# Attention into two gated layers on one core: the first pair's preparation split and fused, turns of an identity ahead of it, the Newton seed on GpSimd, a new table of attention and new last stores

## The chip, the cores and the metric

The kernel runs on one core of one Trainium2 chip. The metric is the device time of one launch in microseconds (us), lower is better; the times shown are the median of three runs, with the lowest and the highest.

## What is computed

```
rmsnorm(x, g) = x / sqrt(mean(x*x) + 1e-6) * g
scores = 1/sqrt(64) * rmsnorm(q, g_q) @ rmsnorm(k, g_k).T      # 4 batches, 12 heads, 448 x 64
attn   = exp(scores - rowmax);  attn /= sum(attn) + 1e-9
x = heads side by side of (attn @ v)                           # 1792 x 768
h = x @ moe_w_in;   x = (h * sigmoid(h)) @ moe_w_out           # 768 -> 2048 -> 768
h = x @ moe2_w_in;  out = (max(h, 0)**2) @ moe2_w_out          # 768 -> 2048 -> 768
```

Everything is float32; the weights arrive as 8-byte floats and are rebuilt into 4-byte ones by bit operations.

## The kernel before

**Stages.** Attention works on 24 pairs of heads, one after the other. `prepare` loads q and k of a pair, squares them (ScalarE, L571), sums the squares (VectorE, L580), finds the inverse root by three Newton rounds from a seed made of the bits of the number (L589 to L625), multiplies (`norm`, L634), turns the result by TensorE transposes (`turn_q`, L646) and cuts it into an upper and a lower part (`q_hi`, L655 and L657, on ScalarE; `q_lo`, L662 and L664, on VectorE). For the first pair the Newton steps run on VectorE, for all others on GpSimd, except the two seed steps L596 and L603, which are always VectorE's. `weigh` makes for each quarter of the rows, or chunk, the score products of both heads (L699), the row maxima (L710), the exponentials (L717), the turn of these (`turn_e`, L726) and a copy out of PSUM (`e_copy`, L525 on ScalarE or L527 on VectorE). `attend` inverts the sums (L746, L747), multiplies with v (L775) and copies the result out of the one PSUM bank `pv` (`pv_copy`, L525). Then layer one (up and down, L1002, L1089, L1186) and layer two (L1089, L1436, L1558), each partly with seven products in place of eight, and the stores of the output (L1422).

**Array forms.** The score products take 64 rows of the array each, so the two heads stand above each other and run at once. The products with v fill 64 columns each and stand side by side. The turns and all products of the layers use the whole array.

**Order.** All work is listed first as steps with the engines that may do them; a planner (`Plan`) then issues them. Attention's steps have fixed times, `nominal`, which is the pair's number times `PERIOD`, plus an entry of `TABLE`, plus for the first four pairs an entry of `FIRST`; on each engine they are issued in the order of these times. All other steps (the loading and splitting of weights, the layers, the stores) go between them where the planner's model finds room, ranked by due times that `DUE` shifts by kind and stage. The numbers end as nothing but the order of each engine's instructions: each engine runs its list in order, and a wait holds back everything behind it.

```
    at = PERIOD * i + {**LOADS, **TABLE}[kind][n] + (FIRST[i][kind][n] if kind in FIRST.get(i, ()) else 0.0)
```

Of the kernel before, what the change touches and what calls it, by code (L numbers as in the profile page):

```python
# [15 lines left out]
P = 128  # L16
# [19 lines left out]
ECOPY = [[("dve",), ("act",)], [("act",), ("dve",)]] * 2  # L36


PERIOD = 10.424
FIT = 0.1  # L40
QUIET = 24.0
LOADS = {
    "load_g": [-27.0], "gains": [-3.0], "load_qk": [-46.9, -46.4], "load_v": [-10.0],
# [3 lines left out]
    "squares": [-25.39, -24.85],  # L47
    "sums": [-21.96],
    "newton": [-18.58, -15.46, -15.21, -14.73, -14.37, -14.0, -13.64, -13.27, -12.91, -12.54, -12.18, -11.81, -11.45, -11.08, -10.72],
    "norm": [-10.35, -7.85],  # L50
    "turn_q": [-8.3, -3.09],
    "q_hi": [-7.71, -2.41],
    "q_lo": [-6.6, -1.71],
    "scores": [0.0, 0.61, 5.21, 5.82],
    "row_max": [0.82, 1.67, 2.75, 2.21, 6.03, 6.57, 7.64, 7.1],
    "exp": [1.47, 3.15, 4.84, 3.76, 6.97, 8.01, 9.77, 9.16],
    "turn_e": [4.25, 4.64, 6.57, 6.95, 9.47, 9.85, 11.78, 12.16],
    "e_copy": [4.85, 5.45, 7.58, 8.18, 11.02, 10.44, 12.82, 14.02],
    "attend": [13.07, 18.28],
    "pv_copy": [21.35],  # L60
    "inverse": [12.09],
    "attended": [22.08],
    "x_hi": [25.45],
    "x_lo": [26.04],
}
FIRST = {
    0: {"squares": [13.08, 13.26], "sums": [11.05], "newton": [8.9, 6.09, 6.15, 7.01, 6.96, 6.9, 6.85, 6.79, 6.79, 6.73, 6.68, 6.67, 6.62, 6.56, 6.51], "norm": [6.45, 4.56], "turn_q": [5.13, 0.65], "q_hi": [5.48, 0.91], "q_lo": [5.05, 0.87], "scores": [-0.12, 0.42, 0.35, 0.89], "row_max": [0.42, 0.11, 1.77, 1.24, 0.89, 0.89, 1.5, 1.5], "exp": [0.43, 0.54, 0.34, 0.55, 0.61, 0.19, 0.22, 0.22], "turn_e": [-1.2, 0.0, 1.44, 1.79, -0.0, 0.0, -0.0, 0.0], "e_copy": [0.21, 0.88, 1.37, 1.5, -0.81, 0.17, -0.31, -0.31], "pv_copy": [0.08], "inverse": [-0.31], "attended": [-0.09], "x_hi": [-0.23], "x_lo": [-0.23]},
    1: {"squares": [4.86, 4.86], "sums": [2.68], "newton": [0.55, -1.24, -0.51, -0.72, -0.71, -0.72, -0.71, -0.72, -0.71, -0.72, -0.71, -0.72, -0.71, -0.72, -0.71], "norm": [0.29, -2.82], "turn_q": [0.2, -3.55], "q_hi": [0.55, -2.22], "q_lo": [0.16, -0.71], "exp": [0.0, -0.0, -0.46, 0.0, 0.72, 0.72, 0.19, 0.19], "turn_e": [0.0, -0.0, 0.38, 0.38, -0.0, 0.0, -0.0, 0.0], "e_copy": [-0.0, -0.22, 0.72, 0.6, -0.58, 0.14, -0.31, -0.31], "pv_copy": [0.23], "inverse": [-0.31], "attended": [0.06], "x_hi": [4.34], "x_lo": [8.92]},
    2: {"squares": [-3.56, -0.81], "sums": [-1.57], "newton": [-2.97, 0.21, 0.21, -0.0, 0.0, -0.0, 0.0, -0.0, 0.0, -0.0, 0.0, -0.0, 0.0, -0.0, 0.24], "norm": [0.24, -1.21], "turn_q": [-0.0, -0.77], "q_hi": [0.0, -0.85], "q_lo": [-0.0, -0.53], "exp": [0.0, -0.0, -0.0, 0.0, -0.0, 0.88, 0.35, 0.34], "e_copy": [-0.0, 0.0, 0.88, -0.0, -0.58, 0.29, -0.31, -0.31], "pv_copy": [0.13], "inverse": [-0.31], "attended": [-0.04], "x_hi": [-0.23], "x_lo": [-0.23]},
# [53 lines left out]
class Plan:  # L123
# [82 lines left out]
    def forward(self, due, end=None):  # L206
# [20 lines left out]
        while len(order) < len(steps):  # L227
            best = None
            for e in ENGINES:
                f = free[e]  # L230
                next = fixed[e][-1] if fixed[e] else None
                for n in wait[e]:
# [170 lines left out]
def kernel(  # L403
# [46 lines left out]
    def sa(shape, dt, tag, n=None):  # L450
        return sb(shape, dt, tag, n, "ap")
# [1213 lines left out]
```

## Time and profile before

| | |
|---|---|
| median of three runs (lowest to highest) | 1171.79 us (1171.0 to 1171.94) |
| time of the profiled execution | 1172.46 us |
| span of its trace, first to last instruction | 1170.6 us |
| TensorE busy | 1147.3 us, 98% |
| VectorE, ScalarE, GpSimd busy | 986.7, 577.7, 298.1 us |
| mean DMA rate | 197 GB/s |

The trace has a line for every instruction with its start and duration. Tile names: `T` holds the split q and k, `n` the normalized ones before the turn, `s`, `t` and `pv` are PSUM banks, `E` the exponentials, `PT` the turned ones, `gg` in the last stage the running sum of the output. PE is TensorE's products, PEld its weight loads, DVE VectorE, ACT ScalarE, POOL GpSimd, SP the engine that issues all DMAs. One fp32 turn or product of v shows as one or two instructions of the array. A line of the timeline that ends in xN is N instructions of one form in a row.

### The profile page before, as it was taken

The page shows a single profiled execution, that of the slowest core. Times are in us where ns is not written, and L with a number is a line of the kernel's source. Part 1 is how long each engine was busy: PE and PEld are TensorE (multiplying, and loading weights), DVE is VectorE, ACT ScalarE, POOL GpSimd, SP SyncE. Part 2 cuts the span into 40 slices and gives each one's busy share as a digit, 9 for nine tenths or more (in the row PEclk, how much of TensorE's full clock was granted, in tenths as well). Part 3 has the DMA queues.
Part 4 walks back from the last instruction along what each step waited for, and adds up shares of the span by engine and source line. Part 5 has one row for each costly group of instructions (what it writes and reads, how often), then busy time and mean ns, then how long its engine had stood idle before and what let it go on. Part 6 is the DMA issues. An engine that isn't in the chain of part 4 may idle for free.

```text
span 1170.6 us, 19174 instructions
## 1 busy us (share of the span) xinstructions
PE 1147.3 (98%) x6825; PEld 1022.6 (87%) x6825; DVE 986.7 (84%) x1737; ACT 577.7 (49%) x1205; POOL 298.1 (25%) x487
## 2 busy tenths in 40 slices
PE   5999999999999999999999999999999999999998
PEld 3777777778899999999999998999999998999997
DVE  7999999887999998995588899678788876888876
ACT  5999999884343333432334353544433534333321
POOL 3566766541000000110010012122341310232220
PEclk9999999999999999999999999999999999999999
DMA  7555547637898888752265839888768795555444
GB/s 172 85 80 92 88 87 108 100 54 175 275 317 236 288 258 283 235 175 70 73 198 189 267 125 310 338 282 293 262 242 289 236 360 212 196 176 185 167 151 146
DMA packets 138720, 230.40 MB, mean 197 GB/s; under 512 B 31616, under 2 KB 102272, under 8 KB 138624
## 3 DMA queue, kind: packets, MB, share of 16 engines
q1 hardware_dynamic: 138624, 229.17, 64.2%
q8 instruction: 54, 0.88, 0.3%
q14 instruction: 42, 0.34, 0.1%
HBM read 154.83 MB, written 74.31 MB: 196 GB/s over the span
## 4 chain that ended last, share of the span: by engine, by line
PE 88%; DVE 7%; DMA 3%; issue 1%; ACT 1%; SPq 0%; DVEq 0%; ACTq 0%
PE s L1186 18%; PE t L1089 16%; PE s L1436 12%; PE t L1002 7%; PE t L726 7%; PE pv L1089 7%; PE pv L775 6%; PE s L1558 6%; PE s L699 6%; PE t L646 2%; DVE w L546 1%; DMA raw<-in_moe_w_in_dram 1%; DVE g L1104 1%; DMA qk<-in_k_dram 0%; DMA v<-sa 0%
## 5 line engine op out<-in xcount | busy, mean ns | idle before, releaser
L1186 PE MATMUL s<-gg,w 128*128 128x448 f32 x1152 | 239.4, 366 | 0.6 <-DVE gg L539 0.3
L1186 PEld LDWEIGHTS s<-gg,w 128*128 128x128 f32 x1152 | 216.0, 188 | 19.8 <-DVE gg L546 1.2
L1436 PE MATMUL s<-w,gh 128*128 128x384 f32 x560 | 142.7, 335 | 1.0 <-DVE gh L539 1.0
L1104 DVE TENSOR_TENSOR g<-t,g 128x448 f32<-128x448 f32 x144 | 86.9, 618 | 58.6 <-PE t L1089 53.3
L717 ACT ACTIVATE E<-s,mx 112x448 f32<-112x448 f32 x192 | 121.8, 645 | 19.7 <-ACT xf L525 12.3
L1452 DVE TENSOR_TENSOR gg<-s,gg 128x384 f32<-128x384 f32 x196 | 102.9, 550 | 28.2 <-PE s L1436 27.9
L1002 PE MATMUL t<-xb,w 128*128 128x448 f32 x576 | 118.8, 365 | 0.0
L1002 PEld LDWEIGHTS t<-xb,w 128*128 128x128 f32 x576 | 108.1, 188 | 8.9 <-issue 0.3
L710 DVE TENSOR_REDUCE mx<-s 112x1 f32<-112x448 f32 x192 | 107.3, 610 | 5.5 <-PE s L699 5.2
L546 DVE TENSOR_TENSOR w<-W,w 128x768 fp32r<-128x768 f32 (+1 forms) x118 | 103.7, 885 | 5.4 <-ACT w L537 4.0
L1436 PEld LDWEIGHTS s<-w,gh 128*128 128x128 f32 x560 | 101.4, 188 | 2.8 <-DVE gh L539 1.4
L726 PEld LDWEIGHTS t<-ident,E 112*112 112x112 f32 x768 | 73.7, 134 | 32.2 <-issue 15.6
L537 ACT CAST w<-W 128x768 fp32r<-128x768 f32 (+1 forms) x71 | 53.6, 759 | 90.5 <-PE s L1186 37.7
L726 PE MATMUL t<-ident,E 112*112 112x112 f32 x768 | 95.4, 266 | 0.7 <-DVE T L662 0.4
L1436 PE MATMUL s<-w,gl 128*128 128x384 f32 x280 | 93.9, 335 | 0.6 <-DVE gl L546 0.6
L1367 ACT ACTIVATE g<-g 128x448 f32<-128x448 f32 x48 | 27.7, 579 | 131.3 <-DVE g L1104 130.9
L775 PE MATMUL pv<-PT,vv 112*64 112x224 f32 x768 | 83.2, 359 | 0.0
L1089 PE MATMUL t<-xb,w 128*128 128x448 f32 x360 | 80.1, 367 | 0.0
L1089 PE MATMUL t<-yb,w 128*128 128x448 f32 x360 | 79.1, 367 | 0.0
L699 PE MATMUL s<-T 64*112 64x448 f32 x576 | 72.7, 383 | 2.3 <-ACT T L655 1.6
L1089 PEld LDWEIGHTS t<-xb,w 128*128 128x128 f32 x360 | 67.4, 188 | 6.3 <-DVE g L1104 0.4
L1089 PEld LDWEIGHTS t<-yb,w 128*128 128x128 f32 x360 | 67.4, 188 | 5.5
(157 smaller groups left out, 2142.4 us busy)
## 6 DMA issues: line engine op xcount, KB each, us to landing
raw<-in_moe_w_in_dram SPq DMA_DIRECT2D x25, 768.0 KB
raw<-in_moe_w_out_dram SPq DMA_DIRECT2D x24, 512.0 KB
su<-w SPq DMA_DIRECT2D x16, 768.0 KB
w<-su SPq DMA_DIRECT2D x16, 768.0 KB
xf<-y SPq DMA_DIRECT2D x48, 224.0 KB
raw<-in_moe_w_out_dram SPq DMA_DIRECT2D x10, 768.0 KB
ki<-W SPq DMA_DIRECT2D x16, 384.0 KB
ko<-W SPq DMA_DIRECT2D x24, 256.0 KB
```

Source lines behind the costliest of these rows:

```text
L546: kind, when, any_t(n, rate), lambda e: engine(e).tensor_tensor(o(), a(), h(), ALU.subtract),
L699: nc.tensor.matmul(pts[j].ap[:CP, :S], T.ap[r, 0, a, c * CP:(c + 1) * CP], T.ap[r, 1, b_], start=(k_ == 0), stop=(k_ == 2),)
L710: lambda e, pt=pt, mx=mx: nc.vector.tensor_reduce(mx.ap, pt.ap[:CP, :S], AX.X, ALU.max, negate=True),
L717: lambda e, j=j, c=c, pt=pt, mx=mx, E=E: nc.scalar.activation(E.ap[:, j], pt.ap[:CP, :S], AF.Exp, bias=mx.ap, accum_out=sums.ap[:, j, c:c ...
L726: nc.tensor.transpose(pe.ap[:CP, m * CP:(m + 1) * CP], E.ap[:, j, m * CP:(m + 1) * CP], ident.ap)
L775: nc.tensor.matmul(pv.ap[j * D:(j + 1) * D, c2 * CT * CP:(c2 + 1) * CT * CP], vr.ap[:, j * NCH + m, :], pt.ap[:, j * NCH + m].rearrange("p ...
L1002: nc.tensor.matmul(pt.ap[:, :S], w_()[:, c, :], x[c // HC].ap[:, a, c % HC, :], start=(c == 0 and n == 0), stop=(c == NC6 - 1 and n == 2),)
L1089: nc.tensor.matmul(pt.ap[:, :S], w_()[:, c0 + c, :], view(b, a, c)(), start=(start and c == 0 and k == 0), stop=(c == HC - 1 and k == 2), ...
L1104: lambda e: nc.vector.tensor_tensor(o.ap, pt.ap[:, :S], a.ap, ALU.add),
L1186: nc.tensor.matmul(pt.ap[:, :S], w_()[:, f, :], gg.ap[:, k, a, f, :], start=(f == 0 and n == 0), stop=(f == HQ - 1 and n == 2),)
L1436: nc.tensor.matmul(pt.ap[:, :NH], g.ap[:, fi, c0:c0 + P], w_()[:, 0, nh * NH:(nh + 1) * NH], start=(n == 0), stop=(n == 5),)
L1452: "acc", at, dve_t(NH), lambda e: nc.vector.tensor_tensor(o(), pt.ap[:, :NH], o(), ALU.add),
```

## The change

In short:

- The first pair's squares are summed in two halves, q's as soon as its squares stand; the seed is one step in place of two; in the first pair each Newton round is three steps in place of four.
- For the other pairs the seed runs on GpSimd, and the addition of a round is written with two operations.
- Forty turns of the identity into the bank `pv` go first on TensorE. Nothing reads them.
- The inverse writes a maximum beside its result (the planner then no longer takes it to keep GpSimd out).
- `PERIOD`, `TABLE`, `FIRST` and `DUE` have new numbers, and a step without a fixed time may enter the DMA queue from the planner's time 13 instead of 24.
- The last 128 rows of the output are made in blocks of 384, 192 and 192 columns, each stored by itself, half of the rows issued by SP and half by ScalarE. Each piece of the output still has one store.

```diff
-PERIOD = 10.424
+PERIOD = 10.386
+WARM = 40
...
-    "attend": [13.07, 18.28],
-    "pv_copy": [21.35],
+    "attend": [11.75, 18.21],
+    "pv_copy": [21.22],
...
+    idle = psum("pv")
+
+    def warm(e):
+        for _ in range(WARM):
+            nc.tensor.transpose(idle.ap[:CP, :CP], ident.ap, ident.ap)
+
+    step("warm", NOW, pe_t(WARM * 0.15), warm, reads=[ident], writes=[idle])
+    plan.fix(0, "warm")
...
+            for n in range(2):
+                step(
+                    "sums", at, dve_t(W2),
+                    lambda e, n=n: nc.vector.tensor_reduce(ms.ap[:, n], sq.ap[:, n], AX.X, ALU.add),
+                    reads=[(sq, n)], writes=[(ms, n)],
+                )
...
-            lambda e: nc.vector.tensor_scalar(
-                ib.ap, ms.ap.bitcast(I32), 1, 0x3FFFFFFF, ALU.logical_shift_right, ALU.bitwise_and),
...
-                y.ap.bitcast(I32), ib.ap, -1.0, float(0x5F3759DF - 0x400000), ALU.mult, ALU.add),
...
+            lambda e: engine(e).tensor_scalar(
+                y.ap.bitcast(I32), ms.ap.bitcast(I32), -0.5, float(0x5F3759DF - 0x400000 - 0x40000000), ALU.mult, ALU.add),
...
+            if not i:
...
+                    lambda e: nc.vector.scalar_tensor_tensor(y.ap, a.ap, 1.5, y.ap, ALU.add, ALU.mult),
...
-                lambda e: engine(e).tensor_scalar(a.ap, a.ap, 1.5, None, ALU.add), writes=[a],
+                lambda e: engine(e).tensor_scalar(a.ap, a.ap, 1.0, 1.5, ALU.mult, ALU.add), writes=[a],
...
-            nc.vector.tensor_scalar(r, r, 1e-9, None, ALU.add)
+            nc.vector.tensor_scalar(r, r, 1e-9, None, ALU.add, ALU.max, accum_out=top.ap)
...
+                    ends = half and fg == NG - 1 and tc_ == TC - 1
+                    blocks = [(0, NH), (NH, NH // 2), (NH + NH // 2, NH // 2)] if ends else [(0, NH), (NH, NH)]
+                    for nh, (e0, en) in enumerate(blocks):
...
+                            on = ("act",) if ends and r0 > c0 else ("sp",)
```

**TensorE in attention.** Half of a pair of the steady part stood so before, twice per pair (`t<-ident,E` is `turn_e`, `t<-ident,n` is `turn_q`, `s<-T` the score products, `pv<-PT,vv` the products with v):

```order
L699 MATMUL s<-T 112x448 x12
L726 MATMUL t<-ident,E 112x112 x8
L646 MATMUL t<-ident,n 128x112 x4
L775 MATMUL pv<-PT,vv 64x224 x8
L726 MATMUL t<-ident,E 112x112 x8
```

A whole pair of the steady part now:

```order
L719 MATMUL s<-T 112x448 x12
L796 MATMUL pv<-PT,vv 64x224 x8
L746 MATMUL t<-ident,E 112x112 x8
L666 MATMUL t<-ident,n 128x112 x4
L746 MATMUL t<-ident,E 112x112 x8
L719 MATMUL s<-T 112x448 x12
L666 MATMUL t<-ident,n 128x112 x4
L746 MATMUL t<-ident,E 112x112 x8
L796 MATMUL pv<-PT,vv 64x224 x8
L746 MATMUL t<-ident,E 112x112 x8
```

The first block of products with v now follows the score products directly. Over all of attention the array goes from one form to another 169 times in place of 190; 23 of these are from score products to products with v.

**ScalarE at the start.** Before, up to the first exponential (`sq<-qk` are squares, `T<-t` the upper parts of the first pair):

```order
L571 ACT_TABLE_LOAD
L571 ACTIVATE sq<-qk 112x512 x8
L657 CAST T<-t 128x448
L655 ACTIVATE T<-t,G 128x448
L717 ACTIVATE E,sum<-s,mx 112x448
```

Now:

```order
L582 ACT_TABLE_LOAD
L582 ACTIVATE sq<-qk 112x512 x5
L677 CAST T<-t 128x448
L675 ACTIVATE T<-t,G 128x448
L582 ACTIVATE sq<-qk 112x512 x2
L737 ACTIVATE E,sum<-s,mx 112x448 x3
```

Three squares of later pairs stood ahead of the first pair's upper parts and now stand behind them.

**VectorE at the start.** Before, from the first pair's `norm` to the first row maxima:

```order
L634 TENSOR_TENSOR n<-qk,y 112x2x4x64 x2
L507 SCALAR_TENSOR_TENSOR G<-graw 128x1
L580 TENSOR_REDUCE ms<-sq 112x16
L664 TENSOR_TENSOR T<-t,T 128x448
L662 SCALAR_TENSOR_TENSOR T<-t,G,T 128x448
L634 TENSOR_TENSOR n<-qk,y 112x2x4x64 x2
L710 TENSOR_REDUCE mx<-s 112x1 x2
```

Now:

```order
L654 TENSOR_TENSOR n<-qk,y 112x2x4x64 x2
L509 SCALAR_TENSOR_TENSOR G<-graw 128x1
L684 TENSOR_TENSOR T<-t,T 128x448
L682 SCALAR_TENSOR_TENSOR T<-t,G,T 128x448
L591 TENSOR_REDUCE ms<-sq 112x16
L730 TENSOR_REDUCE mx<-s 112x1 x2
L654 TENSOR_TENSOR n<-qk,y 112x2x4x64
```

The third pair's sums (L580, now L591) stood ahead of the first pair's lower parts and now stand behind them.

## Rows read from the trace of the kernel before

**Rows 1.** The page: the span.
```profile
span 1170.6 us, 19174 instructions
```
**Rows 2.** Waits of PE, whole span: us in total, times, longest.
```profile
PE t L646 <- POOL y L625: 11.7, 1, 11.7
PE s L1436 <- DVE gh L539: 1.0, 1, 1.0
```
**Rows 3.** Windows by stage: length, PE, PEld, DVE, ACT, POOL busy, PEclk, DMA share, GB/s.
```profile
34.00:256.00 222.00, 221.99 (x2016) 165.95 (x2012) 207.10 (x399) 203.28 (x537) 141.38 (x339) 1.00 0.55 90
273.00:712.00 439.00, 438.52 (x2157) 404.59 (x2157) 372.54 (x600) 173.72 (x286) 33.03 (x22) 1.00 0.67 214
712.00:940.00 228.00, 227.53 (x1196) 215.31 (x1195) 187.65 (x304) 93.01 (x164) 65.11 (x46) 1.00 0.80 284
940.00:1166.00 226.00, 222.93 (x1172) 209.71 (x1170) 178.53 (x354) 75.69 (x142) 45.22 (x38) 1.00 0.56 198
```
**Rows 4.** Timeline of the start: start us, us, engine, line, op [idle before <-releaser].
```profile
5.24 1.22 DVE L580 TENSOR_REDUCE ms<-sq 112x16 f32<-112x1024 f32 x1 [5.24 <-ACT sq L571]
...
8.79 0.17 DVE L621 TENSOR_SCALAR nwt<-nwt 112x16 f32<-112x16 f32 x1
9.00 0.17 DVE L625 TENSOR_TENSOR y<-nwt,y 112x16 f32<-112x16 f32 x1
...
10.88 1.31 DVE L634 TENSOR_TENSOR n<-qk,y 112x512 f32<-112x512 f32 x2
...
11.72 1.73 PE L646 MATMUL t<-ident,n 112*128 112x112 f32 x8 [11.72 <-POOL y L625]
...
12.34 1.67 ACT L571 ACTIVATE sq<-qk 112x512 f32<-112x512 f32 x3 [2.42 <-DVE G L507]
...
14.05 1.22 DVE L580 TENSOR_REDUCE ms<-sq 112x16 f32<-112x1024 f32 x1 [1.77 <-ACT sq L571]
...
14.33 0.63 ACT L655 ACTIVATE T<-t,G 128x448 fp32r<-128x448 f32 x1
...
15.71 0.67 DVE L662 SCALAR_TENSOR_TENSOR T<-t,G,T 128x448 fp32r<-128x448 f32 x1
...
16.44 2.21 PE L699 MATMUL s<-T 64*112 64x448 f32 x10 [0.71 <-DVE T L662]
...
21.76 1.48 PE L699 MATMUL s<-T 64*112 64x448 f32 x12
```
**Rows 5.** The chain of waits, 20 to 41 us: start, length, what.
```profile
20.34 0.75 PE t L646 x4
...
32.52 0.53 PE t L646 x4
...
35.49 0.91 PE t L726 x8
36.40 1.40 PE s L699 x12
...
38.70 0.38 PE t L646 x4
39.09 1.66 PE pv L775 x16
```
**Rows 6.** Timeline of ACT in a steady pair.
```profile
142.50 0.53 ACT L525 COPY PT<-t 112x448 f32<-112x448 f32 x1
142.93 0.54 ACT L525 COPY xf<-pv 128x448 f32<-128x448 f32 x1
```
**Rows 7.** Timeline of DVE at the end.
```profile
1166.00 0.56 DVE L1452 TENSOR_TENSOR gg<-s,gg 128x384 f32<-128x384 f32 x1 [0.49 <-PE s L1436]
```
**Rows 8.** The store's line: count, ns min/median/max, first and last start.
```profile
L1422 SPq DMA_DIRECT2D out_dram<-gg x28: 314/420/1387, 940.5 to 1167.1; - x28
```
**Rows 9.** Windows of the end, columns as in rows 3.
```profile
1168.40:1169.40 1.00, 0.00 (x0) 0.00 (x0) 0.00 (x0) 0.00 (x0) 0.00 (x0) 0.50 0.85 243
1169.40:1170.60 1.20, 0.00 (x0) 0.00 (x0) 0.00 (x0) 0.00 (x0) 0.00 (x0) 0.50 0.00 0
```

More of the change, by code (lines that the diff above doesn't have):

```diff
@@ L46 @@
 TABLE = {
[L47 to L57, printed above, removed]
@@ L58 @@
-    "e_copy": [4.85, 5.45, 7.58, 8.18, 11.02, 10.44, 12.82, 14.02],
-    "attend": [13.07, 18.28],
-    "pv_copy": [21.35],
[L61 to L64, printed above, removed]
+    "squares": [-30.28, -25.74],
+    "sums": [-21.88, -21.23],
+    "newton": [-15.28, -14.92, -14.92, -14.57, -14.23, -13.88, -13.54, -13.19, -12.85, -12.5, -12.16, -11.81, -11.47, -11.12, -10.78],
+    "norm": [-8.23, -5.94],
+    "turn_q": [-6.65, -3.86],
+    "q_hi": [-6.01, -3.12],
@@ L65 @@
+    "q_lo": [-5.04, -2.25],
+    "scores": [0.0, 0.61, 5.17, 5.78],
+    "row_max": [1.35, 0.82, 1.89, 4.1, 5.99, 6.53, 7.07, 8.74],
+    "exp": [2.09, 1.47, 3.16, 4.8, 6.65, 7.79, 8.41, 9.45],
+    "turn_e": [4.22, 4.6, 7.3, 6.91, 9.43, 9.81, 13.74, 13.35],
+    "e_copy": [4.81, 5.96, 9.02, 7.6, 10.41, 10.41, 14.33, 13.95],
+    "attend": [11.75, 18.21],
+    "pv_copy": [21.22],
+    "inverse": [12.82],
+    "attended": [21.78],
+    "x_hi": [23.48],
+    "x_lo": [24.07],
 }
 FIRST = {
-    0: {"squares": [13.08, 13.26], "sums": [11.05], "newton": [8.9, 6.09, 6.15, 7.01, 6.96, 6.9, 6.85, 6.79, 6.79, 6.73, 6.68, 6.67, 6.62, 6.56, 6.51], "norm": [6.45, 4.56], "turn_q": [5.13, 0.65], "q_hi": [5.48, 0.91], "q_lo": [5.05, 0.87], "scores": [-0.12, 0.42, 0.35, 0.89], "row_max": [0.42, 0.11, 1.77, 1.24, 0.89, 0.89, 1.5, 1.5], "exp": [0.43, 0.54, 0.34, 0.55, 0.61, 0.19, 0.22, 0.22], "turn_e": [-1.2, 0.0, 1.44, 1.79, -0.0, 0.0, -0.0, 0.0], "e_copy": [0.21, 0.88, 1.37, 1.5, -0.81, 0.17, -0.31, -0.31], "pv_copy": [0.08], "inverse": [-0.31], "attended": [-0.09], "x_hi": [-0.23], "x_lo": [-0.23]},
@@ L71 @@
+    3: {"squares": [0.16, 0.97], "sums": [0.85, 0.85], "newton": [-4.43, -4.45, -4.45, -4.46, -4.46, -4.47, -4.47, -4.48, -4.48, -4.49, -4.49, -4.5, -3.51, -3.52, -3.52], "exp": [0.0, 0.01, 0.01, 0.0, -0.0, 0.0, -0.0, 0.0], "e_copy": [0.0, 0.06, 0.0, 0.0, 0.07, -0.0, 0.0, -0.0]},
 }
@@ new lines @@
+    "end1": {"acc": -0.25, "h_hi": 17.25, "h_lo": 0.25, "h_sum": -8.25, "join": -9.75, "keep_parts2": 0.25, "load_parts2": -3.75, "load_word2": 1.75, "p1_copy": 14.75, "prod": 10, "square": 5, "store": 5.25, "u_sum": -2.25, "w_hi2": -2, "w_lo2": -5, "w_sum": 9.25, "y_lo": 0.25, "y_sum": 8},
+    "now": {"swap_pools": -14.75},
+    "seg0": {"add": -0.5, "g_lo": 6.5, "keep": 23.75, "keep2": -0.5, "keep_t": -9.5, "load_raw": -13.75, "load_raw2": 0.25, "load_y": 4.5, "low": -7.25, "low2": 13, "magnitude": -3.25, "magnitude2": -2, "out1": -1, "part": -2, "shift": 0.5, "shift2": -2, "sign": 5.75, "sign2": -1, "silu": -2.75, "store_y": -4.75, "w_hi": -2.25, "w_lo": -3.25, "y_hi": 3.5, "y_lo": 4, "y_sum": 2.5},
@@ L244, in forward @@
                         if steps[n].when[0] != "now" and (
-                                st + steps[n].on[e][0] > nx + FIT or st < QUIET and e != "sp"):
+                                st + steps[n].on[e][0] > nx + FIT or st < (QUIET if e != "sp" else LOUD)):
                             continue
@@ L1592, in down @@
                 t += DOWN2 / 2
[L1593 removed]
+                accumulate(total, 2 * self.npair, nh, pt, fg == 0, t, nh * NH, NH)
             return t
```

103 lines of the change are left out of this document (54 added, 49 removed).

## The prediction

> **What bounds the kernel now.** I read the page first, for the span of 1170.6 us [rows 1], then the waits of PE, for what TensorE lacks. It waits 11.7 us for its first product; the largest of its later waits outside the start is 1.0 us, at the end of layer two [rows 2]. The windows by stage say the same from the other side: from 34 to 256 us, the steady part of attention, PE has 221.99 of 222.00 us; the two layers together leave 0.48 + 0.47 + 3.07 = 4.0 us [rows 3]. So four things can move the time: the start, the length of PE's work in a steady pair, those 4.0 us, and the end after the last product. In the steady part VectorE has 207.1 and ScalarE 203.3 of 222 us [rows 3], 93% and 92%: they are close behind PE, so a shorter pair must be checked against them.
>
> **The start.** The timeline [rows 4] gives a chain for the first pair: sums at 5.24, Newton to 10.88, `norm`, first turn at 11.72, second turn's end at 13.45 (11.72 + 1.73), upper part of k at 14.33, lower part of k at 15.71, and only then, at 16.44, the rest of the first score products. Step by step:
>
> 1. Sums in halves. k's squares end when they did, but the sum behind them has 512 elements in place of 1024. Half of 1.22 us with some fixed time is an estimated 0.66: 0.56 us less. q's half lies beside the squares of k.
> 2. Small steps of VectorE follow each other by 0.21 us (8.79, 9.00) [rows 4]. One seed step and three round steps go: 4 x 0.21 = 0.84. The second pair's sums still stand inside the chain, at another place: nothing.
> 3. ScalarE did three squares of later pairs from 12.34 to 14.01 while the turned q and k waited; k's turn had ended at 13.45 and its upper part began at 14.33. Now those squares stand behind: 14.33 becomes about 13.5, 0.8 less.
> 4. VectorE did the third pair's sums from 14.05 on and so reached the lower part of k at 15.71, though the upper part ended at 14.96. Those sums now stand behind: 0.7 less.
>
> Sum: 0.56 + 0.84 + 0.8 + 0.7 = 2.9 us. What was pushed back is late next: the third pair's sums now delay the first row maxima; but the first row maxima come 2.9 earlier than they did, and the same steps lie between them and the steady part, so I carry the whole 2.9. The bounds are 2.0 (the third pair's sums, 1.22, cost most of a us of row maxima) and 3.8 (below). The new order of loads, two weight blocks behind the fifth pair's q and k, costs nothing: layer one starts at 273 us. The issues of q and k on SP now come ahead of those weights and wait for the first `norm`, which is itself earlier.
>
> **The turns of the identity.** Before, the same four turns took 0.75 us at 20.34 and 0.38 us at 38.70 [rows 5], so at the start the engine ran at 1.2 GHz and later at 2.4; the granted clock reads 0.50 after the last product again [rows 9]. Forty turns at 0.75 / 4 take 7.5 us, from about 1.4 us on (the identity has no other input) to 8.9, ahead of the first real turn near 10.3: they are covered. What they can give is the higher clock for the first blocks. For the forecast I take none: between them and the first score products stand some 3 us of little work, and even at the end of the kernel the clock had fallen by 1168.4, after a last product that ended about 1166.0 [rows 7, 9]. The Trainium skill goes the same way: TensorE: Matmul & The Clock Gate, Part 4 (PE-mode transpose), says that the full clock doesn't engage for transposes because they don't count as busy in the same way; by it the turns give nothing ever, and the sum below stands. The trace speaks rather against the page: four blocks of turns stand between the products that ended at 18.65 (16.44 + 2.21) and those at 21.76, and these ran at full speed, twelve in 1.48 us [rows 4].
>
> **A steady pair.** Turns that follow another form take longer: four of `turn_q` 0.53 us right behind score products against 0.38 behind turns, eight of `turn_e` 0.91 behind products with v against 2 x 0.38 [rows 5]. So leaving a form costs 0.15 us. A pair had 2 x (1.40 + 0.91 + 0.38 + 1.66 + 0.91) = 10.52 us with eight changes of form; now it has seven, as the first products with v follow the score products directly. Over all of attention 190 changes become 169: 21 x 0.15 = 3.15 us, taken as 3.1. The trace has no step from score products to products with v. Its price lies between nothing beyond what products with v pay anyway (3.1 saved, or more if they pay less there) and a full leaving besides (23 x 0.15 = 3.45 back, so nothing is saved). I take the former, since the neighbouring rows show the extra time at the return to turns and the direct step has no such return. The Trainium skill, TensorEngine Tiling (Array Packing), Key Properties, says that a change of tiling mode drains the engine; by that rule the direct step is one drain, and 3.1 is right.
>
> VectorE and ScalarE have 15 and 19 of 222 us free [rows 3], 0.7 and 0.9 per pair; a pair shorter by 0.15 fits. VectorE also loses two seed steps of 0.17 per pair and gets a maximum beside the inverse; GpSimd, with 141 of 222 us, takes the seed. Nothing there is on the path.
>
> **The end.** Before: the last sum at 1166.00 takes 0.56 [rows 7], the last store is issued at 1167.1 for about 0.42 [rows 8], data still move at 243 GB/s until 1169.4, and 1.2 us of silence follow [rows 9]. Now the last sum has 192 columns: an estimated 0.36, 0.2 less. Two stores were issued one after the other, now on two engines at once: 0.42 less, of which the data hide a part. Behind the last sum stood 128 x 3072 bytes, 0.39 MB or 1.6 us at 243 GB/s; now it is a quarter, 0.4 us. Against that, twelve short products in place of six: at the 0.095 of a small turn (0.38 / 4) 1.14 us, 0.1 more than now. The 1.2 us stay. Together 1.5 to 1.9; I take 1.5, since no store of this trace was issued by ScalarE. Bounds: 0.4 and 2.0.
>
> **The layers.** Their products are the same; the new due times only reorder. At most 4.0 us are there to win [rows 3]; a loss is bounded by the nearest row, another stage with 3.07 us of idle. The middle is about nothing, and I take nothing.
>
> **Sum.** 2.9 + 3.1 + 1.5 = 7.5 us off the profiled execution's 1172.46 gives 1165.0. The median of the runs, 1171.79, lies 0.67 below that execution, so the forecast for the median is **1164.3 us**.
>
> **The rivals.**
>
> - *The turns of the identity do work.* The clock is up before the first pair and stays. At the low level the rest of the first score products took 2.21 us against 10/12 of 1.40, and four turn blocks 0.75 each against 0.38: 1.0 + 1.5 = 2.5 us, most of it beside VectorE's chain, which doesn't shrink. I take 0.9: 1163.4 us. For it: the full speed at 21.76 after turns alone [rows 4]. Against it: the gap before the first real turn.
> - *The direct step costs a full leaving.* No gain in the steady pair: 1164.3 + 3.1 = 1167.4 us. For it: nobody has seen the step; against it: the rows on where the extra time falls.
> - *The layers lose.* The new due times put a late split of weights or of the squared values ahead of PE for 3 us somewhere, as at the end of layer two now: 1167.3 us.
> - *Slower: the bank of the products with v.* There is one. Between the end of a pair's second block and the next pair's first stood 0.91 + 1.40 + 0.91 + 0.38 = 3.60 us, now 0.91 + 1.40 = 2.31 [rows 5]. Into it must fit the turn of 0.91, an `e_copy` of 0.43 to the next start and the `pv_copy` of 0.54 [rows 6], about 2.0 with the hand-overs: 0.3 to spare. If ScalarE comes later than that, PE stands in every pair. With one exponential (0.62) and one more copy (0.43) ahead, PE waits 0.75 in each of 22 pairs: 16 us, so 1180 us. It decides the sign from some 0.8 us of lateness on. Against it: ScalarE has 0.9 per pair free.
>
> **How the numbers follow.** Chances: the forecast 0.46, turns that work 0.22, the direct step at full price 0.14, layers that lose 0.08, the bank 0.05, others 0.05. About 0.2%, 2.3 us, can be told from no change, so faster means below 1169.4. The first four cases are all faster; two of the losses together (1170.4) are within. That gives faster 0.88, same 0.07, slower 0.05. The low end is the first rival with the upper bound of the end and 2.5 of the layers' 4.0 us: 1163.4 - 0.5 - 2.5 = 1160.4, and half a us for a direct step that is cheaper still: 1159.9. The high end is no gain from the steady pair with the lower bounds of the start and of the end: 1167.4 + 0.9 + 1.1 = 1169.4.
>
> **What would show it.** In the profile after: PE's rest of the first score products near 13.5; four turns there at 0.75 (forecast) or 0.38 us (first rival); a steady pair of about 10.38 us; products with v behind score products at 1.66 and no wait of PE for the `pv_copy`; the end about 3.0 us behind the last product's start of evacuation, not 4.6; idle of PE in the layers near 4 us. A steady pair above 10.5 us would make the prediction wrong.

## The result: 0.8% slower, not 0.6% faster

The changed kernel takes **1181.48 us** (median of 5 runs, 1179.92 to 1183.03) against 1171.79 us before: a ratio of 1.0083, 95% interval 1.0069 to 1.0097. The forecast was 1164.3 us with a range up to 1169.4. The profiled span is 1179.7 us, 9.1 more than before. On the chips of the experiments below times spread further (the kernel before from 1172 to 1193 us), so ratios there have wide intervals and places in the traces decide most questions.

The page and the waits of PE of the changed kernel (us in total, times, longest) answer to [rows 1, 2]:

```profile
span 1179.7 us, 19330 instructions
PE 1158.1 (98%) x6871; PEld 1029.6 (87%) x6871; DVE 966.4 (82%) x1701; ACT 584.6 (50%) x1215; POOL 286.9 (24%) x512
...
PE t L1023 <- ACT g L1035: 4.7, 1, 4.7
...
PE pv L523 <- POOL ident masks.py:199: 1.3, 1, 1.3
PE s L1588 <- ACT gg L1479: 1.2, 1, 1.2
PE s L1463 <- DVE gl L557: 1.2, 1, 1.2
PE pv L796 <- ACT xf L536: 1.1, 1, 1.1
```

After the start, the largest wait of the kernel before was 1.0 us; now one up product of layer one waits 4.7 us for a silu of ScalarE (`g` is what the silu writes; in layer one `gg` is its upper and lower part). The windows of the changed kernel by stage (length, PE, PEld, DVE, ACT, POOL busy, granted clock, DMA share, GB/s) answer to [rows 3]; the short ones were chosen along the granted clock:

```profile
4.80:11.50 6.70, 3.43 (x31) 2.79 (x29) 5.70 (x18) 2.95 (x6) 2.14 (x7) 1.00 0.87 191
11.70:21.70 10.00, 9.16 (x43) 6.72 (x44) 8.40 (x15) 5.87 (x16) 6.57 (x22) 0.50 1.03 279
21.90:34.00 12.10, 11.29 (x103) 8.41 (x102) 10.79 (x22) 11.31 (x31) 6.02 (x17) 1.00 0.18 24
34.00:256.00 222.00, 221.11 (x2002) 164.53 (x2003) 192.53 (x376) 203.25 (x531) 137.06 (x352) 1.00 0.51 90
...
288.10:291.40 3.30, 3.30 (x9) 2.95 (x10) 3.30 (x4) 1.49 (x3) 1.59 (x1) 0.50 0.72 255
500.00:600.00 100.00, 100.00 (x496) 92.69 (x495) 70.75 (x120) 34.13 (x60) 7.94 (x6) 1.00 0.38 127
610.00:700.00 90.00, 90.00 (x437) 81.76 (x436) 74.05 (x118) 33.14 (x54) 10.46 (x8) 1.00 0.53 180
...
940.00:1166.00 226.00, 221.47 (x1154) 206.71 (x1153) 179.94 (x345) 81.71 (x156) 46.20 (x43) 1.00 0.56 198
```

Two things are to be seen. TensorE ran at half clock (1.2 GHz) from about 11.7 to 21.8 us and again from 288.1 to 291.4, right behind the 4.7 us wait. And from 34 to 256 us PE is "busy" 99.6% of the time, though it did 2002 instructions in place of 2016: a busy PE can hide a wait.

I followed single products through both traces; these are the places where 9.1 us came from:

| stretch | before | after | difference |
|---|---|---|---|
| start of the span to the fourth block of score products | 31.05 | 29.53 | -1.5 |
| to the 47th block of score products | 227.61 | 228.98 | +1.4 |
| to the last product of layer one's `gg` (L1186, now L1207) | 469.2 | 476.9 | +7.7 |
| to the first x product of layer two (L1558, now L1588) | 236.0 | 235.6 | -0.4 |
| to the last x product of layer two | 170.8 | 173.7 | +2.9 |
| to the last product of all | 30.9 | 30.8 | -0.1 |
| to the end of the span | 5.0 | 4.1 | -0.9 |

**Layer one.** ScalarE of the changed kernel (timeline: start us, us, line, op [idle before it <- what ended it]):

```profile
278.00 0.83 ACT L548 CAST w<-W 128x768 fp32r<-128x768 f32 x1 [2.20 <-DVE W L938]
285.26 0.89 ACT L922 ACTIVATE W<-raw 128x768 f32<-128x768 f32 x1 [6.42 <-DMA raw<-in_moe_w_in_dram]
286.17 1.28 ACT L1035 ACT_TABLE_LOAD   x1
287.46 0.98 ACT L1035 ACTIVATE g<-t 128x448 f32<-128x448 f32 x2
```

and of the kernel before:

```profile
277.23 0.84 ACT L537 CAST w<-W 128x768 fp32r<-128x768 f32 x1 [2.61 <-DVE W L917]
278.09 1.28 ACT L1014 ACT_TABLE_LOAD   x1
279.94 0.55 ACT L1014 ACTIVATE g<-t 128x448 f32<-128x448 f32 x1 [0.57 <-PE t L1002]
285.23 0.89 ACT L901 ACTIVATE W<-raw 128x768 f32<-128x768 f32 x1 [4.74 <-DMA raw<-in_moe_w_in_dram]
```

The fourth weight block lands at 285.2 in both. Before, the first silu stood ahead of its conversion; now it stands behind it, so the up products run out of the three `t` banks. The load was issued at 273.67 (`raw` on SP's queue) and its conversion began 11.6 us later, where ScalarE had waited 6.4 us for it; the planner's rule for a load (768 KB at 250 to 275 KB per us) makes it some 3 us. Behind the wait come 3.4 us at half clock, 1.7 us lost. The rest of the +7.7: a wait of 1.1 us for `pv_copy` (`xf L536`) at 269.6, and products that ran 2% slower from about 605 to 750 us (products of 448 columns start 206.7 ns apart on average there and 202.7 ahead of it; the rows of 610 to 700 and of 500 to 600 us, with 437 products in 90 us and 496 in 100, show it at a granted clock of 1.00 in both). Summed over its products this stretch cost 2.8 us; before, a short one from about 700 us on cost 0.6. Less some 2 us of small waits of before that are gone, this is the 7.7. Where such a stretch lies differs between executions of one order (the last section), so the sums over the layers below are also given without them.

**Layer two.** The +2.9 us up to the last x product come from the order of the layers and not from one execution: the eight profiles that have the changed attention and the new due times take 173.7 to 173.8 us there, the one with the old due times 170.0, and the four with the layers in the order of before 170.3 to 170.9.

**A steady pair** is 10.65 us (halves of 5.36 and 5.29); before, two halves of 5.27. The direct step from score products to products with v costs nothing extra, as forecast: 132.08 to 133.75, so 1.67 us for the products with v (1.66 in [rows 5]). But in `e e n e e` (`e` is a block of four turns of `turn_e`, `n` one of `turn_q`) the fourth block of turns begins late (timelines of PE and DVE; the four turns of n need 0.38):

```profile
130.67 1.48 PE L719 MATMUL s<-T 64*112 64x448 f32 x12
132.08 1.73 PE L796 MATMUL pv<-PT,vv 112*64 112x224 f32 x16
133.75 0.98 PE L746 MATMUL t<-ident,E 112*112 112x112 f32 x8
134.56 0.55 PE L666 MATMUL t<-ident,n 112*128 112x112 f32 x4
135.15 0.38 PE L746 MATMUL t<-ident,E 112*112 112x112 f32 x2
...
134.38 0.62 DVE L538 COPY PT<-t 112x448 f32<-112x448 f32 x1 [0.80 <-PE t L746]
```

134.56 + 0.38 is 134.94, and the turn starts at 135.15. My theory: with three `t` banks the fourth block of turns in a row needs the first one's bank, and VectorE copies that one only until 135.00. Before, products with v stood between.

### The profile page after: what moved, and what is told of

It is laid out like the page before. It is cut to its first block, busy times and chain, and to the rows that moved or that the text cites. A ratio compares the mean times of both kernels' runs of the same rounds, so it can differ in the third digit from the quotient of the medians.

```text
span 1179.7 us, 19330 instructions
## 1 busy us (share of the span) xinstructions
PE 1158.1 (98%) x6871; PEld 1029.6 (87%) x6871; DVE 966.4 (82%) x1701; ACT 584.6 (50%) x1215; POOL 286.9 (24%) x512
## 3 DMA queue, kind: packets, MB, share of 16 engines
q1 hardware_dynamic: 138704, 228.98, 62.2%
## 4 chain that ended last, share of the span: by engine, by line
PE 73%; DVE 1%; ACT 1%; issue 0%; DVEq 0%; ACTq 0%
PE s L1207 20%; PE t L1110 18%; PE s L1463 12%; PE t L1023 9%; PE pv L1110 7%; PE s L1588 6%; DVE gl L557 0%; DVE g L1520 0%; DVE g L1125 0%; ACT xb L548 0%; ACT g L1388 0%; DVE part L557 0%; DVE gg L1482 0%; DVE w L557 0%; ACT g L1394 0%
## 5 line engine op out<-in xcount | busy, mean ns | idle before, releaser
L1207 PE MATMUL s<-gg,w 128*128 128x448 f32 x1152 | 239.3, 366 | 0.0
L1207 PEld LDWEIGHTS s<-gg,w 128*128 128x128 f32 x1152 | 216.3, 188 | 18.8 <-DVE part L1219 0.2
L1463 PE MATMUL s<-w,gh 128*128 128x384 f32 (+1 forms) x564 | 142.8, 334 | 0.6 <-DVE gh L550 0.5
L1482 DVE TENSOR_TENSOR gg<-s,gg 128x384 f32<-128x384 f32 (+1 forms) x197 | 103.9, 548 | 28.4 <-PE s L1463 27.8
L1023 PEld LDWEIGHTS t<-xb,w 128*128 128x128 f32 x576 | 109.3, 190 | 14.2 <-ACT g L1035 5.1
L730 DVE TENSOR_REDUCE mx<-s 112x1 f32<-112x448 f32 x192 | 110.6, 618 | 7.9 <-PE s L719 7.2
L548 ACT CAST w<-W 128x768 fp32r<-128x768 f32 (+1 forms) x81 | 60.7, 752 | 110.1 <-DVE W L938 39.7
L1463 PEld LDWEIGHTS s<-w,gh 128*128 128x128 f32 x564 | 101.9, 188 | 2.2 <-DVE gh L550 0.9
L1463 PE MATMUL s<-w,gl 128*128 128x384 f32 (+1 forms) x282 | 94.2, 334 | 1.2 <-DVE gl L557 1.2
L538 DVE COPY PT<-t 112x448 f32<-112x448 f32 x96 | 59.5, 620 | 24.1 <-PE t L746 24.1
L557 POOL TENSOR_TENSOR gl<-g,gh 128x448 fp32r<-128x448 f32 (+1 forms) x24 | 25.9, 1079 | 215.2 <-ACT gh L548 121.4
```

Of the source, the lines that this page charges most:

```text
L557: kind, when, any_t(n, rate), lambda e: engine(e).tensor_tensor(o(), a(), h(), ALU.subtract),
L730: lambda e, pt=pt, mx=mx: nc.vector.tensor_reduce(mx.ap, pt.ap[:CP, :S], AX.X, ALU.max, negate=True),
L1023: nc.tensor.matmul(pt.ap[:, :S], w_()[:, c, :], x[c // HC].ap[:, a, c % HC, :], start=(c == 0 and n == 0), stop=(c == NC6 - 1 and n == 2),)
L1207: nc.tensor.matmul(pt.ap[:, :S], w_()[:, f, :], gg.ap[:, k, a, f, :], start=(f == 0 and n == 0), stop=(f == HQ - 1 and n == 2),)
L1463: nc.tensor.matmul(pt.ap[:, :en], g.ap[:, fi, c0:c0 + P], w_()[:, 0, e0:e0 + en], start=(n == 0), stop=(n == 5),)
L1482: "acc", at, dve_t(n), lambda e: nc.vector.tensor_tensor(o(), pt.ap[:, :n], o(), ALU.add),
```

## The experiments

**The due times, and the silu.** The first run takes back the table `DUE`, all five rows of it, and nothing else:

```diff
 DUE = {
...
-    "now": {"swap_pools": -14.75},
+    "now": {"ident": 1.5, "swap_pools": 1},
...
```

> The changed kernel with the old table of due times. The planned order at the start of layer one is the same as in the change (the fourth conversion of a weight block still stands ahead of the first two silu on ScalarE). Theory: the 4.7 us wait at 283 us comes from that order and not from the due times, so it stays; the added idle of layer two's second half (about 2.6 us) comes from the due times and goes: 1181.5 - 2.6 = about 1179 us. Rival: the due times cause both: 1181.5 - 6.4 - 2.6 = about 1172.5 us.

The second only moves the first two silu, with the up products that feed the second, in the planned order; it was run twice:

```diff
         self.span, start, at, order = self.schedule()
+        seg = [n for n in order if self.steps[n].when[0] == "seg"]
+        late = [n for n in seg if self.steps[n].kind == "magnitude"][3]
+        second = [n for n in seg if self.steps[n].kind == "silu"][1]
+        i, j = order.index(late), order.index(second) + 1
+        ahead = [n for n in order[i:j] if self.steps[n].when == self.steps[second].when]
+        order[i:j] = ahead + [n for n in order[i:j] if n not in ahead]
```

> The changed kernel with one reordering on ScalarE: the first two silu stand ahead of the fourth conversion of a weight block (as before the change). Theory: the 4.7 us wait and the 1.7 us lost to the clock that falls behind it go, nothing else moves: 1181.5 - 6.4 = about 1175 us, and in the profile the silu's table load near 279 us. Rival: the weight block itself is late, so TensorE waits for its products a little later for nearly as long: 1179 to 1181.5 us.

> The changed kernel with the first two silu ahead of the fourth conversion of a weight block, once more. Theory: 5.4 us below the changed kernel, a ratio to the kernel before of 1.0037. Rival: most of the stall comes back at the third silu, which still stands behind a conversion: 1.006 to 1.008.

Old due times: 1194.01 us, ratio 1.0154 (1.0108 to 1.0200). Both theories missed the total. The wait for the silu stayed (6.4 us), so it is not the due times'. Layer two's stretch of x products did come back, 170.0 us against 173.7 (170.8 before), so with this attention the due times made that loss. But other waits arose in layer one (1.4 us at 536 us), at the start of layer two (1.2 at 764) and at its end (1.4 at 1173):

```profile
PE t L1023 <- ACT g L1035: 6.4, 1, 6.4
PE s L1463 <- DVE gh L550: 1.4, 1, 1.4
PE pv L1110 <- ACT g L1178: 1.4, 1, 1.4
PE pv L1110 <- ACT g L1388: 1.2, 1, 1.2
```

Silu first: 1182.32 us, ratio 1.0058 (1.0026 to 1.0090), with a profiled span of 1174.3, 5.4 us less than the change's. That looks like the theory, but half of it is the slower products, of which this execution's layer one has none. From the last score product to the last product, without them, it takes 905.5 us, against 908.1 in the change and 900.4 before: the swap itself gives 2.6. Its ScalarE:

```profile
278.94 1.28 ACT L1041 ACT_TABLE_LOAD   x1
280.91 1.15 ACT L1041 ACTIVATE g<-t 128x448 f32<-128x448 f32 x2 [0.69 <-PE t L1029]
287.01 0.90 ACT L928 ACTIVATE W<-raw 128x768 f32<-128x768 f32 x1 [4.96 <-DMA raw<-in_moe_w_in_dram]
```

The wait at the first silu is gone and the clock stays up behind it, so the order on ScalarE made that stall. But the third silu still stands behind a conversion, and PE loses 2.0 us there and 1.8 us later for a late `gg`: 3.8 in place of 6.6 (from start to start; the profile's waits are 1.8, 1.6 and 4.7, with 1.7 of clock behind the last). The up products, no longer held up, reach the late blocks sooner. What is left of the 5.1 us over the kernel before is these 3.8, the 1.1 for `pv_copy` and some 2.3 of layer two, less some 2 of small waits of before that are gone. So each theory has a part, and the rival's is the larger. The repeat on another chip, 1188.67 us and ratio 1.0063 (1.0034 to 1.0091), gives the same: 905.5 us without slower products, with 2.0 and 1.8 us of waits at the same places.

**The clock at the start.** One turn of the identity, and in another run 68:

```diff
-        for _ in range(WARM):
+        for _ in range(1):
```

> The changed kernel with one turn of the identity in place of forty, all else as it is. Theory: the forty turns give nothing, since the clock had fallen again before the first score products: the same within 0.3 us at 30 us, 1181.5 us. Rival 1: they give a part (0.9 us as in the prediction): 1182.4 us. Rival 2: without them the clock rises earlier than 21.8 us, as it rose at 21.5 us in the kernel before, whose work began 1.9 us later: up to 1.5 us faster, 1180 us.

> The changed kernel with 68 turns of the identity in place of forty: at the two durations seen they last until about 9.5 us, just ahead of the first real turn at 9.9. Theory: the clock then stays at its upper level through the first score products and turns, and the blocks from 11.8 to 21.8 us take 1.40 and 0.38 us in place of 2.2 and 0.75: the fourth block of score products starts 1 to 2 us earlier, 1179.5 to 1180.5 us. Rival: the pauses between the first real blocks let it fall all the same, a little later: 1181 to 1181.5 us.

One turn: 1186.27 us, ratio 1.0092 (1.0054 to 1.0129); 68 turns: 1183.49, 1.0076 (1.0038 to 1.0115). The totals cannot tell; the windows and timelines can. The turns of the identity and the first eight real turns with forty (the change), then the real ones with one turn:

```profile
1.33 5.70 PE L523 MATMUL pv<-ident 112*112 112x112 f32 x40 [1.33 <-POOL ident masks.py:199]
9.88 1.21 PE L666 MATMUL t<-ident,n 112*128 112x112 f32 x8 [2.85 <-DVE n L654]
...
10.12 1.75 PE L666 MATMUL t<-ident,n 112*128 112x112 f32 x8 [8.35 <-DVE n L654]
```

A window of the run with one turn, then two of the run with 68:

```profile
9.80:20.80 11.00, 9.22 (x44) 6.83 (x44) 8.57 (x16) 6.37 (x16) 8.14 (x28) 1.00 1.01 272
...
7.60:12.50 4.90, 4.21 (x44) 4.00 (x42) 3.44 (x9) 1.67 (x4) 2.74 (x9) 1.00 1.07 241
12.60:22.00 9.40, 7.03 (x55) 4.97 (x56) 9.38 (x17) 7.51 (x20) 6.09 (x20) 1.00 1.05 285
```

With one turn the first eight real turns take 1.75 us in place of 1.21 and the first score block starts 0.8 later, but the fourth starts at 29.54 (29.53 with forty): of what forty turns give, nothing shows there. The clock came back at 20.9 us with one turn and at 21.8 with forty, so no earlier for them. (The first row's 1.00 is what the records give before their first change; its 44 instructions in 9.22 us are those of half clock.) With 68 turns the blocks run at full clock from 7.6 us on (the twelve score products of the second block take 1.84 us, 17.39 to 19.23, against 2.52) and the fourth block starts at 27.68, 1.9 us earlier, although the first began at 12.59. In three of four later runs with 68 turns the clock fell again at about 15 us, for 3.4 to 6.8 us. So turns up to the first real block carry the clock into the first score products, not always to the end of the start. Nor is 1.9 us what they give each time: the fourth block starts at 28.3 to 29.7 us in the nine profiles with forty turns (median 29.3) and at 27.5 to 29.4 in the five with 68 (median 28.1), so 1.2 us between the medians. One turn has one profile, so a difference of less than a us to forty can't be told.

**The copy behind the fourth turn.** The copy of that one block is cut in half:

```diff
+                h = NCH // 2 if (c, j) == (3, 1) else NCH
                 copy_step(
-                    "e_copy", at, ECOPY[c][j], lambda c=c, j=j: PT[c // CT].ap[:, j * NCH:(j + 1) * NCH, c % CT, :],
+                    "e_copy", at, ECOPY[c][j], lambda c=c, j=j, h=h: PT[c // CT].ap[:, j * NCH:j * NCH + h, c % CT, :],
...
```

> The changed kernel in which VectorE copies only half of the columns of the one turned block whose bank the first turn after the four of turn_q needs; GpSimd sets the other half to zero, so that half of this block's products is left out of the computation. Theory: this copy ends last for that turn, and the hidden wait of 0.2 us in every pair (0.302 us between two turns instead of 0.096) goes with the shorter copy: the longer half of a pair falls from 5.36 to about 5.15 us, a pair from 10.65 to 10.44, the whole by some 21 x 0.2 = 4.2 us to about 1177 us. Rival: the pause belongs to the change from turns of q to turns of e itself (another shape of the turned block, a late weight load): the pair stays at 10.65, 1181.5 us.

The time, 1194.62 us (ratio 1.0134, 1.0086 to 1.0182), doesn't show the copy: in its profile PE waits 7.3 us in attention for `norm` of GpSimd (0 in the change's), behind late transfers and in this run also the zeros that GpSimd sets. The undisturbed halves do show it: 5.19 in place of 5.36, the other 5.28. Its timeline:

```profile
133.19 0.98 PE L748 MATMUL t<-ident,E 112*112 112x112 f32 x8
133.82 0.39 DVE L538 COPY PT<-t 112x224 f32<-112x224 f32 x1 [0.80 <-PE t L748]
134.00 0.55 PE L668 MATMUL t<-ident,n 112*128 112x112 f32 x4
134.39 1.00 PE L748 MATMUL t<-ident,E 112*112 112x112 f32 x8
```

134.00 to 134.39 is 0.39: no wait is left. The bank theory holds. It also shows that without the wait the new order would save 0.07 us in a pair (10.47 against 10.54), not 0.15.

**The old order of the pair.** The old `TABLE`, `PERIOD` and `ECOPY`, with `FIRST` worked out so that the first two pairs and the preparation of the first four stand where the change has them, and the silu moved as above; the second run also has the old due times and 68 turns.

```diff
-PERIOD = 10.386
+PERIOD = 10.424
...
-    "attend": [11.75, 18.21],
+    "attend": [13.07, 18.28],
...
```

> The changed kernel with the old order of the steady pair (the old table from the third pair on; the first two pairs and the preparation of the first four as changed), new due times, and the two silu ahead of the fourth conversion of a weight block. Theory: a half pair takes 5.27 us again in place of 5.36 and 5.29, so 2.2 us over attention; the wait of 1.1 us for the copy of the products with v at its end goes; with the 5.4 us that the silu gave: 1181.5 - 2.2 - 1.1 - 5.4 = about 1173 us. Rival: the planner places the layers anew after another attention, and new waits of 2 to 4 us take their place: 1175 to 1177 us.

> As the run with the old order of the steady pair, with the old due times and 68 turns of the identity. Theory: what the new preparation (1.5 us), the clock that stays up through the start (1.9 us) and the new last stores (0.8 us) give is kept, and nothing is lost in the steady pair or in layer two: 1171.8 - 4.2 = about 1167.6 us, faster than both kernels. Rival: the planner's layer one comes out worse with the old due times, as in the run that had them with the new attention (some 2 to 4 us more of idle there): 1170 to 1172 us.

Halves are 5.27 again in both, and the wait for `pv_copy` at the end is gone (the last product with v starts 7.8 us behind the last score product, 9.6 in the change, 8.0 before). But they took 1182.87 us, ratio 1.0029 (1.0003 to 1.0055), and 1184.69, 1.0039 (1.0015 to 1.0063). The first time fits its rival, though the interval doesn't exclude the theory (1.001); the second lies beyond its rival as well (1.000 at most). The layers decide: they took 905.3 and 910.3 us without slower products, with new waits at other places, in the first run 3.4 us for silu and 1.8 for another product's `g`:

```profile
PE t L1029 <- ACT g L1041: 3.4, 2, 2.1
PE pv L1116 <- ACT g L1394: 1.8, 1, 1.8
PE s L1469 <- DVE gh L556: 1.2, 2, 0.6
```

**The last stores on one engine.**

```diff
-                            on = ("act",) if ends and r0 > c0 else ("sp",)
+                            on = ("sp",)
```

> The changed kernel with all of the last stores issued by SyncE, none by ScalarE; the rest is the same. Theory: the end is set by the transfers that still drain (260 GB/s until 1178 us) and not by the issues, so it stays at 3.8 us from the start of the last sum: 1181.5 us. Rival: the issue is on the path, 0.4 us each: 4.2 to 4.6 us from the last sum, 1181.9 to 1182.3 us.

```profile
1175.87 0.36 DVE L1482 TENSOR_TENSOR gg<-s,gg 128x192 f32<-128x192 f32 x1 [0.31 <-PE s L1463]
...
L1449 ACTq DMA_DIRECT2D out_dram<-gg x3: 552/577/747, 1175.1 to 1176.6; - x3
...
L1449 SPq DMA_DIRECT2D out_dram<-gg x32: 314/426/1027, 951.5 to 1183.9; - x32
```

The first two lines are the change's last sum and ScalarE's stores (ns min/median/max, first and last start), the last one SyncE's stores of this run, whose last sum starts at 1181.51. From the last sum's start to the end it takes 5.4 us, against 3.8 in the change and 4.65 before: the rival's side, and more than it said. In the thirteen other profiles with the new stores on two engines it is 3.8 to 4.0. The smaller stores are six issues, of 0.48 to 0.61 us each, and on one engine the last starts 2.67 us behind the last product (1.07 with two engines, 1.48 before). The total, 1190.59 us (ratio 1.0109, 1.0077 to 1.0141), also holds a stall of 6.7 us for the silu.

**The layers in the order of before.** To take the planner out, its planned places for both layers in the kernel before were written into the kernel as a list, and the order was made from them.

```diff
         self.span, start, at, order = self.schedule()
+        layers = [s.n for s in self.steps if s.when[0] in ("seg", "end") or s.kind == "swap_pools"]
...
+            start[n], at[n] = t / 40.0, ENGINES[e]
...
+        while heap:
+            _, n = heapq.heappop(heap)
+            order.append(n)
...
```

The first run joins it with what gained (new preparation, 68 turns, new last stores) and the old order of the pair; the second has the changed attention; the third is the changed kernel as it is.

> The new preparation of the first pair with 68 turns of the identity and the new last stores; the old order of the steady pair, and both layers in exactly the order that the kernel before has (its planned places are written into the kernel as a list). Theory: everything that was lost comes from the steady pair's order and from the layers' order, so what is left is a gain of 3.5 us at the start (1.5 from the preparation and 1.9 from the clock that stays up) and 0.8 us at the end: 1171.8 - 4.3 = 1167.5 us, faster than both kernels. Rival: an earlier start is given back where the layers begin, as the weight block that they wait for lands no earlier: 1169 to 1171 us.

> The changed kernel, attention included, with both layers in exactly the order of the kernel before. Theory: from the last block of score products to the last product it takes 901 us as before, plus 1.1 us for the wait for the copy of the products with v, in place of 910.9: 1181.5 - 8.8 = about 1172.7 us. Rival: the old order does not fit the new end of attention (three blocks of up products stood ahead of its last products with v), and waits of 2 to 4 us come back: 1175 to 1177 us.

> The changed kernel once more, as a measure for the two others on the same chip. Theory: 1181.5 us, 0.8% over the kernel before. Rival: part of its loss was a matter of one execution (products of 206.7 in place of 202.7 ns from 604 to 742 us): 1179.5 us.

> The version that joins the gains (new preparation with 68 turns, new last stores, old order of the steady pair, old order of the layers), once more. Theory: 4.3 us below the kernel before, a ratio of 0.9963. Rival: part of the gain is given back where loads are late: a ratio of 0.998 to 1.000.

> As the joined version, but with the changed order of the steady pair (68 turns, the new last stores and the old order of the layers as there). Theory: the new attention costs 2.2 us in its steady pairs and 1.1 us at its end, nothing else: 3.3 us above the joined version, a ratio to the kernel before of 0.999. Rival: its end leaves less time between the third weight block's load and the first silu, so the stall of 4 to 7 us comes back with it: 8 to 10 us above the joined version, a ratio of 1.004 to 1.005.

| run | us | ratio to before (interval) | layers, us | without slower products |
|---|---|---|---|---|
| joined version | 1175.58 | 0.9970 (0.9939 to 1.0001) | 899.9 | 899.8 |
| joined version, again | 1176.17 | 0.9953 (0.9924 to 0.9982) | 901.6 | 901.0 |
| changed attention, old layers | 1192.20 | 1.0100 (1.0054 to 1.0147) | 917.3 | 908.7 |
| the same with 68 turns | 1192.23 | 1.0090 (1.0059 to 1.0121) | 908.9 | 908.8 |
| the change | 1192.03 | 1.0129 (1.0068 to 1.0190) | 910.7 | 910.7 |

(Layers: from the last score product to the last product; 901.0 us before, 900.4 without slower products.) The joined version comes out ahead of both kernels, and of the kernel before by 0.3% (the interval just reaches 1) and 0.5%, where 0.37% was expected; the span of its first profile is 1167.8 us. The changed attention with the same layers does not: it went the rivals' way and beyond them (1.010 and 1.009, where they said 1.003 to 1.005). Two things of it show in the profile of the run with 68 turns, its waits of PE and a stretch of GpSimd (L764 is `norm`, L929 the product of `xf` with the turned inverse `R`):

```profile
PE t L776 <- POOL n L764: 11.4, 9, 3.2
PE t L1133 <- ACT g L1145: 6.3, 1, 6.3
...
190.76 0.22 POOL L755 TENSOR_TENSOR y<-nwt,y 112x16 f32<-112x16 f32 x1
197.50 1.13 POOL L929 TENSOR_TENSOR xf<-xf,R 128x448 f32<-128x448 f32 x1 [6.51 <-DMA R<-rd]
198.58 2.04 POOL L764 TENSOR_TENSOR n<-qk,y 112x512 f32<-112x512 f32 x2
...
199.68 1.01 PE L776 MATMUL t<-ident,n 112*128 112x112 f32 x4 [3.19 <-POOL n L764]
```

First, where `R` comes late, GpSimd waits in order and the `norm` behind it comes late too. In the changed order that `norm` is turned 1.95 us after it ends (132.61 to 134.56 in the change's profile); before, the one behind the product was turned 4.2 us after (135.11 to 139.34). The joined version, on the same chip and in turn with this run, lost 0.3 us to `norm`. `R` came late for it too, but less in sum: GpSimd stood idle ahead of these products for 59.6 us within attention, 79.2 there, with 7.9 and 7.8 us as the longest. From 34 us on, over all profiles, PE lost 0 to 0.7 us to `norm` in the four with the old order of the pair (0 in the kernel before) and 0 to 11.4 in the eleven with the changed one. But the larger losses go with the larger idle sums, and runs of both orders with about 60 us of idle lost 0.3 to 0.7, so how much of the 11.4 us is the order's stays open. Second, the wait for the silu is back with the layers in their old order: here the third weight block was issued 7.0 us behind the start of the last block of score products (4.5 before and in the change) and converted at 19.9 (10.2 before), and the silu stands behind it. So the change's attention ends in a way that the old layers don't fit; the order and the loads must be placed together. All runs keep the seed on GpSimd and the maximum beside the inverse, and none takes back the earlier entry into the DMA queue by itself: what these do alone isn't shown.

## Why the prediction was wrong

The forecast took 7.5 us off, the profile after has 9.1 more. Of the 16.6 us between them the layers make 10.1 (from the 47th block of score products on, 2.2 of them slower products), the steady pair 4.5, the start 1.4 and the end 0.6. The prediction's own sign of being wrong, a steady pair above 10.5 us, is there: 10.65.

- **The start: 2.9 us forecast, 1.5 measured.** The chain did better than its four terms: the rest of the first score products starts at 12.52, not 13.5 (16.44 before), as `norm` came 1.75 us earlier and the first eight turns took 1.21 us in place of 1.73. The second score block comes 3.9 us earlier. Then 2.4 of these are lost up to the fourth block, most of it since everything from 11.7 to 21.7 us ran at half clock. "The same steps lie between them and the steady part, so I carry the whole 2.9" was the step that failed: before, the clock rose just ahead of the second block, so that block and what followed it ran at full speed; now they began earlier than the clock did. The clock is not all of it: with 68 turns and the clock up the second block comes 4.4 us earlier and the fourth 3.4, so 1.0 is lost there too. And 1.5 is one execution: the nine profiles with forty turns give 1.4 to 2.8.
- **The turns of the identity: 0 forecast, nothing measured at the fourth block**, but not because turns can't raise the clock. Forty turns and nothing else took 3.4 us for the first 18 and 2.3 us for the other 22, so they ended at full clock; it fell at about 11.6 us, after 4.6 us with little but eight turns. The Trainium skill, TensorE: Matmul & The Clock Gate, Part 4 (PE-mode transpose), which says that transposes don't raise the clock, is contradicted here. The gap, the forecast's own reason, was right, and the run with 68 turns shows what filling it can give: 1.9 us there, 1.2 between the medians of all runs.
- **The steady pair: -3.1 us forecast, +1.4 measured.** The direct step was priced rightly. The Trainium skill, TensorEngine Tiling (Array Packing), Key Properties, has one drain for it, and 1.67 us against 1.66 agrees. Two steps failed. Saving one change of form was taken as 0.15, and without the wait a pair saves 0.07 (10.47 with the half copy, 10.54 before). And I checked `e e n e e` against VectorE's and ScalarE's totals ("a pair shorter by 0.15 fits"), not against the three banks: the fourth block in a row waits 0.2 us for a copy. I looked at the one `pv` bank as a rival and not at the three `t` banks.
- **The `pv` bank**, priced at 16 us if it decided, cost 1.1 us once, at the end of attention. Its break-even, "some 0.8 us of lateness", doesn't follow from its own numbers: 7.5 us over 22 pairs is 0.34, with the 0.3 to spare 0.64.
- **The end: -1.5 forecast, -0.8 measured.** The smaller sum came as forecast (0.36). The step that failed is the data, "now it is a quarter, 0.4 us" in place of 1.6: from the last issue to the last packet it took 2.4 us before and takes 1.6 now, 0.7 less and not 1.2, and the silence behind it, which was to stay at 1.2, is 1.4. The issues gave half of their 0.42, which was the median of all stores (the last two before took 0.48 and 0.60): three on each engine take 0.48 to 0.75 us apiece, so the last begins 1.07 us behind the last product, 0.41 earlier than before (1.48), and 0.2 of that is the smaller sum.
- **The layers: 0 forecast, +9.9 measured (910.9 against 901.0), +7.7 without slower products (908.1 against 900.4, the wait for `pv_copy` among them; 2.4 of it in layer two).** I called "the layers lose" a rival at 3 us with 0.08; it was the main case. The bound was the step that failed: "a loss is bounded by the nearest row, another stage with 3.07 us of idle". A bound from idle of the old order says nothing of a new order. The planned order of the change has the conversion ahead of the silu on ScalarE, and the trace of before has the fourth load's conversion waiting 4.74 us; the two put together would have shown 285.2 as the earliest silu.

## What to carry to other kernels

When a planner places the work anew, look for in-order engines whose next instruction waits for a transfer, and ask what now stands behind it: here 4.7 us of stall and 1.7 of clock hung on one swap on ScalarE, and in one run 11 us on a `norm` behind a late transfer on GpSimd. Undoing one such swap gives back less than the stall, since the next late transfer then shows. Count PSUM banks along each run of blocks between two that use another bank; a busy share of 100% hides such waits, intervals between starts don't. A gain at the start is worth what is left of it when the clock and the next stage have been counted.

## What was not expected of the hardware

In layer one products of 448 columns start 202.7 ns apart and, for some 145 us, 206.7, at the same granted clock of 1.00 (windows of 500 to 600 and 610 to 700 us above); with the same order such a stretch lay from about 275 to 613 us in another execution (68 turns; 6.3 us), with the silu first nowhere or mostly from 318 to 614, and in the run with the old layers it cost 8.6 us. It is no level of its own: from layer two's first product of L1436 on (743 us; now L1463, 750 us), the slower pace is the usual one in all 16 profiles, the kernel before included (206.3 ns on average there, 206.0 in the change). What it comes from stays open; it is larger than most of the effects in question, so spans were compared only where it was taken out or the same. A 768 KB load took 5.6 us from issue to its conversion in one place (268.08 to 273.70) and 12.2 in the next (273.02 to 285.23) of the kernel before.
